# Attention products with v in column tiles of 32, and sums of both heads in the same rows

## The chip, the cores and the metric

The kernel runs on one core of one Trainium2 chip. The metric is the device time of one execution in microseconds; the kernel before has a median of 639.19 us over three runs (638.57 to 639.40).

## The reference

Three layers follow one another. The diff touches only the first, attention over 2 x 8 heads of width 64 with 576 pooled queries and 1152 keys a head; its output goes through a routed expert layer and a last gated layer.

```python
q_pool = q.reshape(B, H, S // 2, 2, D).mean(axis=3)
scores = np.matmul(q_pool, k.transpose(0, 1, 3, 2)) / np.sqrt(D)
scores = scores - np.max(scores, axis=-1, keepdims=True)
attn = np.exp(scores)
attn = attn / (np.sum(attn, axis=-1, keepdims=True) + 1e-09)
x = np.matmul(attn, v)
...
x = moe(x)
...
out = (h * np.tanh(softplus(h))) @ w_out      # h = x @ w_in
```

## The kernel before

Attention handles the 16 heads as 8 pairs (p = 0 to 7), and the keys of a pair as 9 tiles of 128 (t = 0 to 8). The main loop runs over the 72 steps (p, t). Each step issues the scores of its tile (keys on partitions, queries along the free dimension, lines 320 and 322), ACT exponentiates them into the tile `Pt[p, t]`, and some matmuls of the next pair's row maxima stand between (`max_chunk`, lines 237 and 241). All orders are written out by hand; each engine runs its instructions in that order.

The products with v don't run at every step. `groups` collects three tiles: at steps 0, 3 and 6 the products of the three tiles before are issued. At step 0 they are the last three of the pair before, and its end. In the last pair groups have two tiles, at steps 2, 4, 6 and 8, and the last tile stands alone behind the loop.

`pv(p, t, f)` multiplies exp(scores) of half f of the 576 queries with v: for each of the two heads, one matmul with 128 keys as contraction, 64 columns of weights (the width of v) and 288 queries as the moving operand. Head h writes rows 64h to 64h + 63 of PSUM bank f (`pvt[p][f]`), columns 0 to 287. VectorE adds the tiles of a group into `St`, and `psums` then sums exp(scores) over the keys: matmuls whose weights are `e2[:, h]`, 32 columns, all zero but column h, which is one. They write columns 288 to 447 of the same banks, 160 queries at a time. Operands are float32.

At the end of a pair `evac_x` lets ACT copy the products of bank f out of PSUM (the tile is `wd` in the trace), `evac_s` lets ACT copy the sums of the second head, and `sum_both` lets VectorE add the sums of the first head onto them (`sm`), so that both heads' sums stand in one set of rows. `sum_log` (line 401, weights of 32 columns) forms gate products at step 3 (step 4 in the last pair) between products and sums; at step 6 the transposes of the next pair's maxima stand there (`max_rows`, lines 287 and 289). `sum_tr` transposes `sm` at step 6.

Line numbers: 339 is the matmul of `pv`, 371 that of `psums`, 473 the transposes of the finished products; 90 (ACT) and 93, 96, 99, 102 (VectorE, POOL) are helpers.

Of the kernel before, what the change touches and what calls it, by code (L numbers as in the profile page):

```python
# [15 lines left out]
ALU = mybir.AluOpType  # L16
# [5 lines left out]
B, H, S, D = 2, 8, 1152, 64  # L22
SQ = S // 2
HQ = SQ // 2
# [6 lines left out]
KT = S // P  # L31
# [52 lines left out]
def kernel(ctx, tc, cst, qt, kt, v, wgo, w1, w2, wio, out):  # L84
    nc = tc.nc
    V, A, G, T, SP = nc.vector, nc.scalar, nc.gpsimd, nc.tensor, nc.sync
    mm = T.matmul

    def act(out, in_, func=AF.Copy, **kw):
        A.activation(out=out, in_=in_, func=func, **kw)  # L90

    def tt(eng, out, a, b, op):
        eng.tensor_tensor(out=out, in0=a, in1=b, op=op)  # L93
# [55 lines left out]
    sm = ap.tile([P, 384], F32, name="sm")  # L149
# [8 lines left out]
    kd, qd, vt, At, QS, QB, xut = {}, {}, {}, {}, {}, {}, {}  # L158
    Pt, pvt = {}, {}
# [68 lines left out]
    def max_chunk(p, h, j, c):  # L228

        pool, name = (mxp, "mx") if p or c == 0 else (scp, "sc")  # L230
        ps = pool.tile([P, 512], F32, name=name)[:, :KC]

        def keys(g_):
            return KD[p, g_] if c == 1 else At[p, g_][:, c * KC:(c + 1) * KC]

        if j < 4:
            mm(ps, lhsT=QS[p, h][:, j * P:(j + 1) * P], rhs=keys(h), start=True, stop=True)  # L237
        else:

            for g_ in range(2):  # L240
                mm(ps, lhsT=QM[p % 2][:, g_ * P:(g_ + 1) * P], rhs=keys(g_), start=g_ == 0, stop=g_ == 1)
        if c == 0:
            red(Mp[p % 2][:, h, j, 0:1], ps, ALU.max)
        elif c == 1:

            i, nrl[0] = nrl[0] % 3, nrl[0] + 1
            rlt[p, h, j] = wd[13 + i][:, (640, SQ, 0)[i]:(640 + KC, SQ + KC, KC)[i]]
            act(rlt[p, h, j], ps, AF.Relu)
        else:
            r_ = rlt.pop((p, h, j))  # L250
            V.tensor_tensor_reduce(out=r_, in0=ps, in1=r_, scale=1.0, scalar=-3.0e38, op0=ALU.add, op1=ALU.max, accum_out=Mp[p % 2][:, h, j, 1:2])  # L251
# [8 lines left out]
    def step_chunks(p, t):  # L260

        if p == 0 and t < 6:
            return [(1, *units[u], c) for u in FIRST[t] for c in (0, 2)], [(1, *units[u], 1) for u in FIRST[t + 1]]
        n, u = (p + 1, t + 3) if t < 6 else (p + 2, t - 6)
        if n >= NPAIR:
            return [], []
        unit = lambda i, c: (n, *units[i], c)
        if t % 3 == 0:
            post = [unit(u, 0), unit(u, 2), unit(u + 2, 1)]
            return [unit(u, 1), unit(u + 1, 1)], [post[i] for i in ((0, 2, 1) if t == 6 else (0, 1, 2))]  # L270
        return [unit(u, 0), unit(u, 2)], []
# [29 lines left out]
    last = NPAIR - 1  # L301
# [8 lines left out]
    def scores(p, t):  # L310
        ks = slice(t * P, (t + 1) * P)
        Pt[p, t] = ap.tile([P, 2, SQ], F32, name="pt", bufs=4)
        pool, name = (mxp, "mx") if other(p, t) else (scp, "sc")
        s0 = pool.tile([P, 512], F32, name=name)
        s1 = [pool.tile([P, 512], F32, name=name)[:, :SQ - F0] for h in range(2)]
        lo, hi = slice(0, F0), slice(F0, SQ)

        def part(o, h, qs_, low, first=True, last_=True):
            if low:
                mm(o, lhsT=Bt[(2 * p + h) % NBL][:66, ks], rhs=QB[p, h][:66, qs_], start=False, stop=last_, skip_group_check=not (first and last_))  # L320
            else:
                mm(o, lhsT=At[p, h][:, ks], rhs=QS[p, h][:, qs_], start=first, stop=False, skip_group_check=not (first and last_))  # L322

        for low in (False, True):
            part(s1[0], 0, hi, low)
        act(Pt[p, t][:, 0, F0:], s1[0], AF.Exp, scale=0.0625)
        for low in (False, True):
            for h in range(2):
                part(s0[:, h * F0:(h + 1) * F0], h, lo, low, h == 0, h == 1)
        act(Pt[p, t][:, :, :F0], s0.rearrange("p (h n) -> p h n", h=2), AF.Exp, scale=0.0625)  # L330
        for low in (False, True):
            part(s1[1], 1, hi, low)
        act(Pt[p, t][:, 1, F0:], s1[1], AF.Exp, scale=0.0625)

    def pv(p, t, f):
        if t == 0 and f == 0:
            pvt[p] = [pvp.tile([P, 512], F32, name=f"pv{i}") for i in range(2)]
        for h in range(2):
            mm(pvt[p][f][64 * h:64 * h + 64, :HQ], lhsT=vt[p][:, t, h, :], rhs=Pt[p, t][:, h, f * HQ:(f + 1) * HQ], start=t == 0, stop=t == KT - 1, skip_group_check=True)  # L339


    St = {}
# [1 line left out]
    def groups(p, t):  # L344

        if p == last and t:
            return [(last, i) for i in range(t - 2, t)] if t % 2 == 0 else []
        g = 9 * p + t
        return [divmod(i, KT) for i in range(g - 3, g)] if t % 3 == 0 and g else []

    def add_tile(tiles):
        p = tiles[0][0]
        if len(tiles) > 1:
            St[p] = ap.tile([P, 2, SQ], F32, name="st", bufs=1)
            tt(V, St[p], Pt[tiles[0]], Pt[tiles[1]], ALU.add)
            if whole(tiles):
                tt(V, St[p], St[p], Pt[tiles[2]], ALU.add)

    def whole(tiles):
        return len(tiles) == 3 and tiles[0] != (0, 0)  # L360

    def psums(tiles):
        p = tiles[0][0]
        srcs = [St[p]] * (len(tiles) > 1) + [Pt[tiles[-1]]] * (len(tiles) != 2 and not whole(tiles))
        end = tiles[-1][1] == KT - 1
        for f in range(2):
            for src in srcs:
                for h in range(2):
                    for a in range(2):
                        q_, t0 = 64 * h + 32 * a, 256 * a + 160 * f  # L370
                        mm(pvt[p][f][q_:q_ + 32, HQ:HQ + 160], lhsT=e2[:, h], rhs=src[:, h, t0:t0 + 160], start=False, stop=end and src is srcs[-1], skip_group_check=True)

    def evac_x(p, f):
        b, hp = divmod(p, 4)
        xu = xut[p] = wd[14][:, :SQ]
        act(xu[:, f * HQ:(f + 1) * HQ], pvt[p][f][:, :HQ])
        if f:
            o = 512 if b == 0 else 0
            G.tensor_copy(xu4[:, hp, 64 * b:64 * b + 64], xu[:, o:o + 64])

    def evac_s(p):
        b = p // 4
        sr = sm[64:, 64 * b:64 * b + 320].rearrange("p (f n) -> p f n", f=2)
        for f in range(2):
            act(sr[:, f], pvt[p][f][64:, HQ:HQ + 160])

    def sum_both(p):
        b = p // 4
        sr = sm[64:, 64 * b:64 * b + 320].rearrange("p (f n) -> p f n", f=2)
        for f in range(2):  # L390
            tt(V, sr[:, f], pvt[p][f][:64, HQ:HQ + 160], sr[:, f], ALU.add)

    rct, slt = {}, {}

    def sum_log(p, out=True):

        b, hp = divmod(p, 4)
        ps = bank(now[0])
        for a in range(2):
            qs_ = slice(256 * a, 256 * a + 320)  # L400
            mm(ps[32 * a:32 * a + 32, :320], lhsT=wbd[:, hp], rhs=xut[p][:, qs_], start=True, stop=True)
        slt[p] = ps
        if out:
            evac_l(p)

    def evac_l(p):
        b = p // 4
        act(sm[:64, 64 * b:64 * b + 320], slt[p][:64, :320])
# [184 lines left out]
    for p in range(NPAIR):  # L593
        n, m = p + 1, p + 2
# [144 lines left out]
    def run(g, slot):  # L739
        for f in sched.get((g, slot), ()):  # L740
            f()

    for g in range(9 * NPAIR):
        p, t = divmod(g, 9)
        now[0] = g
        scores(p, t)
        run(g, 0)
        pre, post = step_chunks(p, t)
        for c_ in pre:
            max_chunk(*c_)  # L750
        tiles = groups(p, t)
        if tiles:
            add_tile(tiles)
        run(g, 1)
        end = tiles and tiles[-1][1] == KT - 1
        for f in range(2):
            for i in tiles:
                pv(*i, f)
            if end:
                evac_x(p - 1, f)  # L760
        if t == 6 and p < last:
            max_rows(p + 1)
        if p and t == (4 if p == last else 3):
            sum_log(p - 1)
        if tiles:
            psums(tiles)
        run(g, 4)
        if end:
            evac_s(p - 1)
        run(g, 2)  # L770
        for c_ in post:
            max_chunk(*c_)
        if end:
            sum_both(p - 1)
        run(g, 3)
    psums([(last, KT - 1)])
    for f in range(2):
        pv(last, KT - 1, f)
        evac_x(last, f)
    sum_log(last, False)  # L780
    evac_s(last)
    sum_both(last)
    evac_l(last)
    sum_tr(last)
    sum_last(last)
# [543 lines left out]
    for q, (n_, i, _, main, w_, _) in enumerate(flat):  # L1329
# [39 lines left out]
        elif wq and (n_ == 5 and i % 2 or n_ == 6 or n_ == 7 and i < 4) and len(ws2) < NPRE:  # L1369
            f = len(ws2)  # L1370
# [300 lines left out]
```

## Time and profile before

| | |
|---|---|
| median of three runs | 639.19 us |
| profiled execution | 640.59 us |
| its span, first to last instruction | 638.8 us |
| mean granted TensorE clock | 0.988 |
| TensorE busy (PE) | 612.3 us, 96% |
| VectorE (DVE) | 500.6 us, 78% |
| ScalarE (ACT) | 393.1 us, 62% |
| GpSimd (POOL) | 256.4 us, 40% |

PE is the matmuls, PEld the weight loads beside them. Busy times of records that overlap are counted once. The attention stage lasts to about 258 us of the span.

### The profile page before, as it was taken

To read this page: it belongs to the slowest core of one execution; us is meant where nothing else is said; L and a number is where in the kernel's file an instruction comes from. 1 tells how busy PE (TensorE), PEld (TensorE's weight loads), DVE (VectorE), ACT (ScalarE), POOL (GpSimd) and SP (SyncE) were. 2 spreads that over 40 slices of the span, in tenths; PEclk is the share of its full clock that TensorE was granted. 3 is DMA by queue.
4 is the path that set the end of the run, shared out by engine and by line. 5 is a ranking of instruction groups with operands and counts; after the bars stand their busy time and mean duration, and the time that the engine had idled before them with its cause. 6 is when DMAs were issued, how large, how long until landed. Compare 5 with 4: busy or idle time off the path is not lost.

```text
span 638.8 us, 11233 instructions
## 1 busy us (share of the span) xinstructions
PE 612.3 (96%) x4041; PEld 488.3 (76%) x4041; DVE 500.6 (78%) x1018; ACT 393.1 (62%) x855; POOL 256.4 (40%) x236
## 2 busy tenths in 40 slices
PE   8999999999999999599999989999999999999996
PEld 4677877768777766289868768597979998999993
DVE  7769798888888888558846768757898778878775
ACT  7888888888887674244555465844654545554453
POOL 6766738565566342242215132103323332223221
PEclk9999999999999999699999999999999999999999
DMA  8685745555451321498797694920000200010001
GB/s 325 201 230 186 214 144 126 159 148 192 91 177 48 111 89 65 142 334 295 267 388 265 239 374 195 331 73 2 0 1 1 100 2 1 2 43 7 1 0 54
DMA packets 27341, 89.73 MB, mean 140 GB/s; under 512 B 2854, under 2 KB 7599, under 8 KB 23186
## 3 DMA queue, kind: packets, MB, share of 16 engines
q1 hardware_dynamic: 22176, 74.80, 33.0%
q0 software_dynamic: 3504, 8.65, 5.9%
q10 hardware_dynamic: 1602, 5.51, 2.6%
q8 instruction: 34, 0.56, 0.4%
q14 instruction: 25, 0.20, 0.1%
HBM read 79.51 MB, written 9.84 MB: 140 GB/s over the span
## 4 chain that ended last, share of the span: by engine, by line
PE 65%; DVE 16%; ACT 8%; issue 4%; DMA 4%; POOL 1%; SPq 0%; ACTq 0%; DVEq 0%
PE pv L339 10%; PE ops L1489 8%; PE mx L237 5%; PE sc L322 5%; PE sc L320 5%; DVE l L96 4%; PE zps L1027 3%; PE zps L1028 3%; PE zps L1029 3%; PE yp L1027 2%; PE yp L1029 2%; PE yp L1028 2%; DVE n L96 2%; ACT l L90 2%; PE hps L1196 2%
## 5 line engine op out<-in xcount | busy, mean ns | idle before, releaser
L99 POOL TENSOR_SCALAR u<-u 128x384 f32<-128x384 f32 x46 | 58.8, 1279 | 143.5 <-ACT u L90 136.6
L90 ACT ACTIVATE pt<-sc 128x320 f32<-128x320 f32 (+1 forms) x198 | 87.9, 491 | 10.1 <-PE sc L320 7.6
L90 ACT ACTIVATE l<-n,two 128x384 f32<-128x384 f32 x48 | 29.6, 616 | 80.5 <-DVE n L96 80.5
L339 PE MATMUL pv<-pt,vt 128*64 128x288 f32 x576 | 75.6, 411 | 0.0
L322 PE MATMUL sc<-qs,at 128*128 128x320 f32 (+1 forms) x264 | 67.3, 299 | 0.0
L320 PE MATMUL sc<-qb,Bt 66*128 66x320 f32 (+1 forms) x264 | 66.6, 296 | 0.0
L339 PEld LDWEIGHTS pv<-pt,vt 128*64 128x64 f32 x576 | 39.0, 137 | 28.5 <-issue 5.2
L102 DVE TENSOR_REDUCE Mp<-mx 128x1 f32<-128x384 f32 x72 | 39.9, 556 | 24.9 <-PE mx L237 19.5
L1028 PE MATMUL zps<-yh,wd 128*128 128x384 f32 x176 | 59.1, 336 | 0.0
L1489 PE MATMUL ops<-wd,gh 128*128 128x512 f32 x135 | 53.2, 394 | 0.0
L99 POOL TENSOR_SCALAR dm<-dm 128x512 f32<-128x512 f32 x21 | 42.8, 2039 | 22.7 <-ACT dm L90 22.6
L96 DVE SCALAR_TENSOR_TENSOR l<-n,r 128x384 f32<-128x384 f32 x48 | 26.7, 557 | 31.1 <-ACT r L90 31.1
L322 PEld LDWEIGHTS sc<-qs,at 128*128 128x128 f32 x264 | 46.1, 189 | 1.0 <-issue 0.8
L93 POOL TENSOR_TENSOR Bt<-kd,at 64x576 fp32r<-64x576 f32 x32 | 46.3, 1461 | 0.2
L320 PEld LDWEIGHTS sc<-qb,Bt 66*128 66x128 f32 x264 | 45.3, 189 | 0.0
L93 DVE TENSOR_TENSOR w2l<-wt,w2h 128x512 fp32r<-128x512 f32 x32 | 25.9, 815 | 15.9 <-ACT w2h L90 15.7
L237 PE MATMUL mx<-at,qs 128*128 128x384 f32 x120 | 36.1, 369 | 1.5 <-DVE qs L93 0.8
L93 DVE TENSOR_TENSOR st<-pt 128x1152 f32<-128x1152 f32 x25 | 35.8, 1431 | 1.3 <-ACT pt L90 1.3
L1065 POOL DMA_INDIRECT ybuf<-y,six x11 | 11.2, 1020 | 63.7 <-ACT y L90 62.1
L93 DVE TENSOR_TENSOR n<-n,l 128x384 f32<-128x384 f32 x48 | 34.8, 725 | 1.7
L251 DVE CUSTOM_DVE_ANT_0 wd<-mx,wd 128x384 f32<-128x384 f32 x63 | 34.6, 550 | 1.8 <-PE mx L237 1.6
L1028 PEld LDWEIGHTS zps<-yh,wd 128*128 128x128 f32 x176 | 33.0, 188 | 1.5
(364 smaller groups left out, 1719.2 us busy)
## 6 DMA issues: line engine op xcount, KB each, us to landing
wt<-in_w SPq DMA_DIRECT2D x32, 1024.0 KB, 8.0
kd<-in_kt SPq DMA_DIRECT2D x16, 576.0 KB, 5.2
wraw<-in_wio SPq DMA_DIRECT2D x11, 512.0 KB, 4.5
wd<-in_wio SPq DMA_DIRECT2D x11, 512.0 KB, 4.1
vt<-in_v SPq DMA_DIRECT2D x8, 576.0 KB, 6.3
wraw<-in_wio ACTq DMA_DIRECT2D x7, 512.0 KB, 5.4
tq<-in_qt SPq DMA_DIRECT2D x12, 288.0 KB, 4.4
tq<-in_qt POOLq DMA_DIRECT2D x12, 288.0 KB, 6.4
```

The lines of the kernel that those rows point to most:

```text
L90: A.activation(out=out, in_=in_, func=func, **kw)
L93: eng.tensor_tensor(out=out, in0=a, in1=b, op=op)
L96: V.scalar_tensor_tensor(out=out, in0=a, scalar=s, in1=b, op0=op0, op1=op1)
L99: eng.tensor_scalar(out=out, in0=a, scalar1=s1, scalar2=s2, op0=op0, op1=op1)
L102: V.tensor_reduce(out=out, in_=in_, axis=AX.X, op=op)
L237: mm(ps, lhsT=QS[p, h][:, j * P:(j + 1) * P], rhs=keys(h), start=True, stop=True)
L251: V.tensor_tensor_reduce(out=r_, in0=ps, in1=r_, scale=1.0, scalar=-3.0e38, op0=ALU.add, op1=ALU.max, accum_out=Mp[p % 2][:, h, j, 1:2])
L320: mm(o, lhsT=Bt[(2 * p + h) % NBL][:66, ks], rhs=QB[p, h][:66, qs_], start=False, stop=last_, skip_group_check=not (first and last_))
L322: mm(o, lhsT=At[p, h][:, ks], rhs=QS[p, h][:, qs_], start=first, stop=False, skip_group_check=not (first and last_))
L339: mm(pvt[p][f][64 * h:64 * h + 64, :HQ], lhsT=vt[p][:, t, h, :], rhs=Pt[p, t][:, h, f * HQ:(f + 1) * HQ], start=t == 0, stop=t == KT - 1, ...
L1028: mm(out_, lhsT=b_, rhs=c, start=False, stop=False)
L1489: mm(opt[b_, j], lhsT=(g_, g_, gl_)[i], rhs=(wo, wl_, wo)[i], start=f == 0 and i == 0, stop=f == NF - 1 and i == 2)
```

## The change

Each product with v is split into two of 32 weight columns, so the four column tiles of bank f are written by head 0 and head 1 with two each. In `psums` the loop over bank f moves inside the loop over the head, and the row block of a sum is chosen by the bank (64 f) and no longer by the head (64 h): both heads add into the same rows, where the weights keep them in different rows of the block. `evac_s` therefore reads rows 64 f of bank f, and `sum_both` is dropped with both of its calls.

```diff
         for h in range(2):
-            mm(pvt[p][f][64 * h:64 * h + 64, :HQ], lhsT=vt[p][:, t, h, :], rhs=Pt[p, t][:, h, f * HQ:(f + 1) * HQ], start=t == 0, stop=t == KT - 1, skip_group_check=True)
+            for d in range(0, D, 32):
+                mm(pvt[p][f][64 * h + d:64 * h + d + 32, :HQ], lhsT=vt[p][:, t, h, d:d + 32], rhs=Pt[p, t][:, h, f * HQ:(f + 1) * HQ], start=t == 0, stop=t == KT - 1, skip_group_check=True)
...
-        for f in range(2):
-            for src in srcs:
-                for h in range(2):
+        for src in srcs:
+            for h in range(2):
+                for f in range(2):
                     for a in range(2):
-                        q_, t0 = 64 * h + 32 * a, 256 * a + 160 * f
+                        q_, t0 = 64 * f + 32 * a, 256 * a + 160 * f
                         mm(pvt[p][f][q_:q_ + 32, HQ:HQ + 160], lhsT=e2[:, h], rhs=src[:, h, t0:t0 + 160], start=False, stop=end and src is srcs[-1], skip_group_check=True)
...
-            act(sr[:, f], pvt[p][f][64:, HQ:HQ + 160])
-
-    def sum_both(p):
-        b = p // 4
-        sr = sm[64:, 64 * b:64 * b + 320].rearrange("p (f n) -> p f n", f=2)
-        for f in range(2):
-            tt(V, sr[:, f], pvt[p][f][:64, HQ:HQ + 160], sr[:, f], ALU.add)
+            act(sr[:, f], pvt[p][f][64 * f:64 * f + 64, HQ:HQ + 160])
...
-        if end:
-            sum_both(p - 1)
...
-    sum_both(last)
```

## Rows read from the trace of the kernel before

**Rows 1.** The page: TensorE's busy time, and the chain's shares by line.
```profile
PE 612.3 (96%) x4041; PEld 488.3 (76%) x4041; DVE 500.6 (78%) x1018; ACT 393.1 (62%) x855; POOL 256.4 (40%) x236
...
PE pv L339 10%; PE ops L1489 8%; PE mx L237 5%; PE sc L322 5%; PE sc L320 5%; DVE l L96 4%; PE zps L1027 3%; PE zps L1028 3%; PE zps L1029 3%; PE yp L1027 2%; PE yp L1029 2%; PE yp L1028 2%; DVE n L96 2%; ACT l L90 2%; PE hps L1196 2%
```

**Rows 2.** Windows of attention: stretch, length, busy us (count) of PE, PEld, DVE, ACT, POOL; clock.
```profile
26.00:228.00 202.00, 198.14 (x1608) 149.87 (x1606) 171.28 (x377) 166.69 (x387) 120.97 (x110) 1.00 0.52 153
228.00:256.00 28.00, 27.83 (x270) 18.59 (x269) 24.50 (x46) 15.12 (x36) 9.18 (x5) 1.00 0.30 92
```

**Rows 3.** Waits of TensorE, 26 to 256 us: total us, times, longest.
```profile
PE mx L237 <- ACT qb L90: 1.3, 6, 0.2
...
PE mx L237 <- DVE Mp L102: 0.3, 1, 0.3
```

**Rows 4.** Lines 339 and 371: records, ns min/median/max, first and last start.
```profile
L339 PE MATMUL pv<-pt,vt x576: 406/406/458, 30.0 to 255.7; 128*64 128x288 f32 x192
...
L371 PE MATMUL pv<-st,e x400: 299/299/324, 33.1 to 253.8; 128*32 128x160 f32 x134
```

**Rows 5.** Time line of TensorE, first sums: start, length, record count.
```profile
33.35 0.45 PE L371 MATMUL pv<-pt,e 128*32 128x160 f32 x8
...
33.89 0.46 PE L371 MATMUL pv<-pt,e 128*32 128x160 f32 x8
```

**Rows 6.** Time line of TensorE, a pair's end (step 0).
```profile
110.16 3.13 PE L339 MATMUL pv<-pt,vt 128*64 128x288 f32 x24
113.22 0.48 PE L371 MATMUL pv<-st,e 128*32 128x160 f32 x8
113.86 0.48 PE L371 MATMUL pv<-st,e 128*32 128x160 f32 x8 [0.16 <-ACT wd L90]
```

**Rows 7.** The last round of the products in that group.
```profile
112.88 0.41 PE L339 MATMUL pv<-pt,vt 128*64 128x288 f32 x2
```

**Rows 8.** Time line of TensorE at a step 3.
```profile
122.38 0.47 PE L371 MATMUL pv<-st,e 128*32 128x160 f32 x4
122.64 0.44 PE L401 MATMUL mx<-wd,wbd 128*32 128x320 f32 x2
```

**Rows 9.** Time line of TensorE at a step 6.
```profile
103.50 0.75 PE L371 MATMUL pv<-st,e 128*32 128x160 f32 x16
...
104.84 0.44 PE L237 MATMUL mx<-kx,qs 128*128 128x384 f32 x1 [0.21 <-ACT qb L90]
```

**Rows 10.** Time line of ACT at the end of that pair.
```profile
113.40 0.41 ACT L90 ACTIVATE wd<-pv 128x288 f32<-128x288 f32 x1 [1.10 <-PE pv L339]
...
115.12 0.49 ACT L90 ACTIVATE wd<-mx 128x384 f32<-128x384 f32 x1 [0.21 <-PE mx L237]
```

**Rows 11.** VectorE's additions of the sums, by shape: busy us, mean ns, idle before.
```profile
L93 DVE TENSOR_TENSOR sm<-pv,sm 64x160 f32<-64x160 f32 x16 | 4.5, 314 | 3.0 <-ACT sm L90 2.9
```

**Rows 12.** The chain of the last pair: start, length, what.
```profile
232.51 0.68 ACT dm L90
...
236.28 2.44 POOL dm L99
238.74 0.44 DVE dm L99
...
251.90 1.36 DVE st L93
...
253.31 0.75 PE pv L371 x16
```

**Rows 13.** Time line of all engines at the end of attention.
```profile
254.25 0.75 PE L371 MATMUL pv<-pt,e 128*32 128x160 f32 x16
254.93 1.19 PE L339 MATMUL pv<-pt,vt 128*64 128x288 f32 x8
...
256.94 0.55 DVE L93 TENSOR_TENSOR sm<-pv,sm 64x160 f32<-64x160 f32 x2 [2.29 <-ACT sm L90]
...
257.47 0.43 ACT L90 ACTIVATE sm<-sc 64x320 f32<-64x320 f32 x1 [0.38 <-PE sc L401]
```

## The prediction

> **What bounds the kernel now.** I read the page's engine line first, then the windows around the attention stage (the only stage that the diff touches), the waits of TensorE in it, the chain, and last the time line of TensorE around each kind of group. The page says that TensorE is busy for 96% of the span and that the line of the products with v holds 10% of the chain [rows 1]. The windows split attention in two. From 26 to 228 us TensorE works 198.1 of 202.0 us at a granted clock of 1.00, and nothing else is as full; from 228 to 256 us, the last pair of heads, it is again full, but VectorE is at 24.5 of 28.0 [rows 2]. The largest kind of wait that TensorE has in all these 230 us comes to 1.3 us [rows 3]. So up to 228 us a nanosecond saved or added on TensorE moves everything behind it; after 228 us the chain has to be asked again (below).
>
> **How the product groups run.** 8 pairs x 9 key tiles x 2 halves x 2 heads are 288 matmuls of the program; the trace has 576 records of them, so each leaves two [rows 4], and records of two column tiles run side by side. The lengths 406 ns for 288 columns and 299 ns for 160 [rows 4] differ by 107 ns for 128 columns, 0.836 ns a column: 288 columns stream in 241 ns, 160 in 134. A group of three key tiles starts at 110.16, its last round at 112.88 [rows 6, 7]: 11 intervals, less 0.052 (458 - 406) for the uncovered first weight load [rows 4], give 0.2425 us a round of two records: streaming and 2 ns. The sums already use four column tiles of 32. Rows of two rounds each start at 33.35 and 33.89, four rounds apart [rows 5]: 0.135 us a round of four records, again streaming and some 2 ns. Hence four streams side by side cost no more than two.
>
> **Part 1, tiles of 32 columns.** The records double to 1152, but four now share a round: 1152/4 = 576/2 = 288 rounds of the same 288 columns. Change: 0, on the evidence of the sums' rounds. The doubled issuing is covered too: the two-source sums issue 16 matmuls of the program in 8 rounds of 0.135 (one in 68 ns), while the new products need 24 in 12 rounds of 0.2425 (one in 121 ns). Not shown is a round of four with 288 columns: the bound below is 0, as nothing can stream faster; above, I take the start stagger as uncovered, 28 - 14 ns more a round. That stagger I get from the first two rows of the sums: the records of rows 4 with 299 ns give a two-round row of 0.45 (0.135 + 0.299 + three staggers), so about 7 ns each; 288 x 14 ns = 4.0 us. I take 0, the row that is nearest in kind.
>
> **The switch that goes.** From the last round of the products (112.88) to the first of the sums (113.22) pass 0.34 us [rows 6, 7], a round and 0.10 more. Where both have 32 columns I take that 0.10 away, and the sums' uncovered first load, 324 - 299 = 25 ns [rows 4]. The products' own uncovered first load falls from 52 ns to what 32 columns cost in the sums, 25: 27 ns less. A group whose products are followed directly by 32-column work gains 0.10 + 0.025 + 0.027 = 0.152 us. Of the 21 groups up to 228 us and at the start of the last pair, 7 are at step 3 of a pair (in six the gate product of line 401 stands between, also of 32 columns [rows 8]): 7 x 0.152 = -1.06. Seven are at step 6: between products and sums stand the transposes of the row maxima, 34 columns, so both switches stay and only 27 ns are gained (the wait on ACT's qb behind them [rows 9] follows the transposes, so it moves too): 7 x 0.027 = -0.19.
>
> **What the new order of the sums costs.** The other seven are at step 0, the end of a pair, and they wait. Before, the four sums of bank 0 run at once (113.22), then those of bank 1 wait until ACT has emptied the products of bank 1 (ACT 113.40 for 0.41) and start at 113.86 [rows 6, 10]. The new loop has bank inside head: two sums of bank 0, then two of bank 1 that wait for the same ACT instruction, and queued behind them on TensorE are the second head's two of bank 0 and two of bank 1. After the release there were 8 records in two rounds, 0.48 us [rows 6]. Now there are 12, and those of one bank lie in only two column tiles: head 0 then head 1 in bank 1 is four rounds in the same tiles, as long as a whole undisturbed group, 0.75 us [rows 9]. So 0.75 - 0.48 = +0.27, less the 0.027 of the first load: +0.245 a group. It can't be more, as four rounds are all the work there is; it would be 0 if TensorE took the later head around the held instruction. I take +0.27, because a waiting instruction is followed by nothing of its line in any of these groups.
>
> **Part 2, additions gone.** 16 additions on VectorE, 4.5 us busy [rows 11]. Up to 228 us TensorE waits for VectorE 0.3 us in all [rows 3], so they were hidden under its matmuls and free nothing; bounds 0 and -0.3. At the end of attention they run 256.94 to 257.49, while ACT copies the gate sums from 257.47 to 257.90 [rows 13], and the transposes need both: 0. ACT's two copies of the sums stay. The first now waits for the fourth round too, but ACT stood idle 0.21 us behind the copies, waiting for TensorE [rows 10], and that moves with TensorE: 0.
>
> **The last pair.** The chain there goes over ACT, POOL and VectorE, not TensorE: ACT's dm at 232.51 behind the copies of the sums, POOL's clamp 236.28 to 238.72, then from 238.74 to the addition at 251.90 thirty pieces, all VectorE's or its issuing; that addition releases the sums at 253.31 [rows 12]. The +0.245 of this pair's step 0 enters that chain through the copies of the sums; the gains of 0.152 at its steps 2, 4 and 6, and at 8 where VectorE is awaited, are eaten by it: 0 for the four. Behind it the last products follow sums directly: 254.93 - 254.25 is 0.68 [rows 13], against 0.54 for four rounds in one mode plus a first load 0.025: 0.115 gone, and 0.052 of first load with it: -0.165.
>
> **Sum.** -1.06 - 0.19 + 7 x 0.245 (1.72) - 0.165 = +0.30 us. The profiled execution took 640.59, its span 638.8 with 1.8 us around it: 640.9. It lay 1.40 above the median of the runs shown, 639.19, so I forecast a median of 639.5. About 0.2% (1.28 us) is what a measurement of this kernel can tell from no change.
>
> **Rivals.**
> - The hold at the end of a pair costs nothing, as TensorE runs the second head around the held sums. For it: behind line 401's first round four records of the sums start at 122.38 in other column tiles, before that line's second round [rows 8]. Against: those were not held by a wait. 7 x 0.27 less: 640.9 - 1.9 = 639.0, median 637.6, faster by 0.25%.
> - Rounds of four at 288 columns don't close up: the fourth stream's start stagger is added to each round. For it: no row shows four streams that long. Against: at 160 columns nothing is added. It decides from (1.28 - 0.30)/288 = 3.4 ns a round; at 14 ns, 639.5 + 4.0 = 643.5.
> - VectorE's freed 4.5 us are worth something in the last pair, where it is the chain. Against: it starts behind POOL there. Elsewhere TensorE waits 0.3 us for VectorE [rows 3], which I take as its bound: 639.2, within the likeliest's range.
>
> The Trainium skill, TensorEngine Tiling (Array Packing), section Instruction Overhead, says that each matmul carries about 60 cycles of overhead and warns of small ones; that speaks against doubling the count. At 2.4 GHz that is an estimate of 25 ns, for 576 added records 14.4 us if none of it is covered, 653.9; rounds of four that last 0.135 us [rows 5] don't show it.
>
> **Chances and range.** Likeliest (the sum) 0.69, by itself 638.7 to 640.4, which is the scatter of the runs (638.57 to 639.40) around it; no hold 0.12; rounds of four lengthened 0.10 (the uncovered overhead in it 0.02); the rest, 0.09, is a shift of ACT at pair ends that costs another 0.27 each (641.4), or small gains inside the likeliest's range. From 637.3 to 641.4 leaves out little more than the lengthened rounds. Faster by over 0.2%: 0.13; within: 0.69; slower: 0.18.
>
> **What would show it.** 1152 records of line 340 in 288 rounds of 0.2425; last products to first sums 0.24 instead of 0.34 at steps 3; at step 0 sums that end 0.27 later after ACT's evacuation; VectorE some 4.5 us less busy; span 638.8 + 0.3. Wrong if a round of four exceeds 0.246, if sums of the second head start before the evacuation ends, or if a pair's steps 1 and 2 wait for ACT where they didn't.

## The result, and the profile after

The changed kernel takes 642.98 us (median of 6 runs, 642.17 to 644.17), the kernel before beside it 638.85 (638.37 to 639.40): ratio 1.0064, 95% interval 1.0052 to 1.0077. The forecast was 639.5 within 637.3 to 641.4, so the time lies outside its range, on the slow side. The same kernel was measured four more times beside the kernel before, with ratios 1.0000, 1.0048, 1.0027 and 1.0047 (below). The mean of the five is 1.0037, some 2.4 us: the change loses, but by less than its first measurement says.

The page of the changed kernel, its engine line and two DMA queues (queue, kind: packets, MB, share):

```profile
PE 611.6 (95%) x4617; PEld 487.6 (76%) x4617; DVE 493.8 (77%) x1002; ACT 393.2 (61%) x855; POOL 257.4 (40%) x236
...
q8 instruction: 38, 0.62, 0.4%
q14 instruction: 25, 0.20, 0.1%
```

Against [rows 1] TensorE has 576 records more and less busy time, and VectorE 16 instructions and 6.8 us less. The two last lines I had passed over: transfers of the kind "instruction", 16 KB each on q8 and 8 KB on q14. They turn out to matter most.

The windows of attention in the changed kernel, to compare with [rows 2], and two behind attention:

```profile
26.00:228.00 202.00, 196.86 (x2084) 148.41 (x2082) 166.75 (x364) 166.11 (x386) 121.29 (x110) 1.00 0.52 153
228.00:256.90 28.90, 27.96 (x369) 18.97 (x369) 24.16 (x44) 16.00 (x38) 9.71 (x5) 1.00 0.28 89
272.00:276.00 4.00, 1.84 (x13) 1.39 (x12) 1.38 (x2) 1.20 (x2) 1.79 (x2) 0.93 0.83 244
276.00:280.00 4.00, 4.00 (x25) 4.00 (x24) 1.95 (x4) 1.63 (x3) 0.00 (x0) 0.63 0.78 235
```

TensorE now idles 5.1 us of the first 202 instead of 3.9. In the last two windows it stands idle for half of four microseconds and then works four at a granted clock of 0.63, a mixture of 1.2 and 2.4 GHz; in the kernel before the clock of 276 to 280 us is 1.00.

The lines of the products and the sums, for [rows 4]:

```profile
L340 PE MATMUL pv<-pt,vt x1152: 406/406/431, 30.0 to 256.5; 128*32 128x288 f32 x192
...
L372 PE MATMUL pv<-st,e x400: 299/299/324, 32.9 to 254.7; 128*32 128x160 f32 x134
```

TensorE's time line at the end of the pair of [rows 6], and at the step 3 behind it, for [rows 8]:

```profile
110.60 3.12 PE L340 MATMUL pv<-pt,vt 128*32 128x288 f32 x48
113.54 0.44 PE L372 MATMUL pv<-st,e 128*32 128x160 f32 x4
114.31 0.74 PE L372 MATMUL pv<-st,e 128*32 128x160 f32 x12 [0.33 <-ACT wd L90]
...
119.98 3.12 PE L340 MATMUL pv<-pt,vt 128*32 128x288 f32 x48
122.92 0.44 PE L396 MATMUL mx<-wd,wbd 128*32 128x320 f32 x2
122.93 0.47 PE L372 MATMUL pv<-st,e 128*32 128x160 f32 x4
```

From the first product to what follows pass 2.94 us (110.60 to 113.54, and 119.98 to 122.92): 12 rounds of 0.2425 and a first load of 0.03. Before it was 3.06 (110.16 to 113.22). The sums of bank 1 wait for ACT and 12 records follow in 0.74. Both are as the prediction had them. So the loss has to be elsewhere, and two places show it. The first stands between pair 0 and pair 1, on ACT's time line and then TensorE's, in the changed kernel:

```profile
42.44 0.70 ACT L90 ACTIVATE at<-kd 128x576 fp32r<-128x576 f32 x1
44.30 0.68 ACT L90 ACTIVATE qs<-tq 128x576 fp32r<-128x576 f32 x1 [1.16 <-DMA tq<-in_qt]
...
46.35 0.44 PE L237 MATMUL mx<-kx,qs 128*128 128x384 f32 x1 [0.67 <-ACT qb L90]
```

In the kernel before the same two rows are

```profile
43.44 0.68 ACT L90 ACTIVATE qs<-tq 128x576 fp32r<-128x576 f32 x1
...
46.06 0.44 PE L237 MATMUL mx<-kx,qs 128*128 128x384 f32 x1 [0.21 <-ACT qb L90]
```

ACT waits 1.16 us for the accumulating load of a query tile (`tq`, issued by POOL at 36.1), and hands the delay to TensorE's matmuls of the maxima. The second place is behind attention, at the first expert, which waits for gathered tokens; each row is the transposes of one of the first three gathered tiles, in the changed kernel:

```profile
271.81 0.75 PE L992 MATMUL xps<-cs,xg 128*128 128x128 f32 x4
273.02 0.63 PE L992 MATMUL yp<-cs,xg 128*128 128x128 f32 x4 [0.46 <-DMA xg<-xbuf,gix]
275.35 1.00 PE L992 MATMUL yp<-cs,xg 128*128 128x128 f32 x4 [1.71 <-DMA xg<-xbuf,gix]
```

and the third in the kernel before:

```profile
273.55 0.66 PE L1000 MATMUL yp<-cs,xg 128*128 128x128 f32 x4 [0.93 <-DMA xg<-xbuf,gix]
```

The second tile came 1.0 us later than in the kernel before (whose attention ended 0.8 us earlier), the third 1.8 us. The wait and the slow clock behind it are the two odd windows above.

### The profile page after: what moved, and what is told of

Its sections match the earlier page's. It is cut to its first block, busy times and chain, and to the rows that moved or that the text cites. A ratio compares the mean times of both kernels' runs of the same rounds, so it can differ in the third digit from the quotient of the medians.

```text
span 642.0 us, 12368 instructions
## 1 busy us (share of the span) xinstructions
PE 611.6 (95%) x4617; PEld 487.6 (76%) x4617; DVE 493.8 (77%) x1002; ACT 393.2 (61%) x855; POOL 257.4 (40%) x236
## 4 chain that ended last, share of the span: by engine, by line
PE 60%; DVE 17%; ACT 8%; DMA 7%; issue 5%; POOL 2%; SPq 0%; ACTq 0%; DVEq 0%; POOLq 0%
PE pv L340 8%; PE ops L1481 8%; PE sc L322 4%; PE sc L320 4%; DVE l L96 4%; PE mx L237 4%; PE zps L1019 3%; PE zps L1020 3%; PE zps L1021 3%; DMA tq<-in_qt 2%; DVE n L96 2%; PE yp L1019 2%; PE yp L1021 2%; PE yp L1020 2%; ACT l L90 2%
## 5 line engine op out<-in xcount | busy, mean ns | idle before, releaser
L340 PE MATMUL pv<-pt,vt 128*32 128x288 f32 x1152 | 75.2, 408 | 0.0
L340 PEld LDWEIGHTS pv<-pt,vt 128*32 128x32 f32 x1152 | 34.9, 110 | 31.5 <-issue 4.7
L99 POOL TENSOR_SCALAR dm<-dm 128x512 f32<-128x512 f32 x21 | 43.2, 2057 | 22.5 <-ACT dm L90 22.4
L237 PE MATMUL mx<-at,qs 128*128 128x384 f32 x120 | 36.1, 369 | 1.2 <-DVE Mp L102 0.6
L93 DVE TENSOR_TENSOR w2l<-wt,w2h 128x512 fp32r<-128x512 f32 x32 | 24.5, 771 | 12.0 <-ACT w2h L90 11.8
```

The source lines that it names most:

```text
L99: eng.tensor_scalar(out=out, in0=a, scalar1=s1, scalar2=s2, op0=op0, op1=op1)
L340: mm(pvt[p][f][64 * h + d:64 * h + d + 32, :HQ], lhsT=vt[p][:, t, h, d:d + 32], rhs=Pt[p, t][:, h, f * HQ:(f + 1) * HQ], start=t == 0, sto ...
```

## The experiments

Eighteen kernels ran. The starts of the groups of products in each profile were set against those of the kernel before; "end of attention" is the first of the last pair's own gate products, behind the loop (256.63 us before, 257.45 after; "the first gate product" below), counted from pair 0's step 3, so that differences of the loads at the start drop out.

**Halves of the change, and an early guess.** `e1` has the products of 32 columns with the old sums; `e2` the new sums with products of 64; `e3` is the kernel before, with 28 matmuls of 64 columns more ahead of its last products.

```diff
 # e2, against the changed kernel
-            for d in range(0, D, 32):
-                mm(pvt[p][f][64 * h + d:64 * h + d + 32, :HQ], lhsT=vt[p][:, t, h, d:d + 32], ...
+            mm(pvt[p][f][64 * h:64 * h + 64, :HQ], lhsT=vt[p][:, t, h, :], ...
 # e3, against the kernel before
+    for _ in range(7):
+        for q_ in range(0, P, 32):
+            mm(pvt[last][0][q_:q_ + 32, 448:], lhsT=e2[:, 0], rhs=Pt[last, KT - 1][:, 0, :64], ...)
```

> Products in tiles of 32 columns, sums and additions as before. Theory A (the loss has two parts: the sums of bank 1 held at the pair ends, and a loss of 2 to 3 us behind attention that depends only on when attention ends): every group keeps its gain and none pays the longer hold, so the last gate product of attention, 256.63 us before, comes at about 255.1, and the time is 636.5 to 638.5. Theory B (column tiles of 32 cost something by themselves that the attention stage does not show, for instance through the doubled instruction stream): attention ends as early, but the time stays above that of the kernel before, about 641.

> Products in tiles of 64 columns as before, sums by bank and half with both heads in the same rows, no additions. Theory A: seven pair ends pay 0.27 us each and nothing is gained, so the last gate product comes at about 258.5 instead of 256.63, and the time is 641 to 643. Theory B: the attention stage is later by the same 1.9 us, but nothing is lost behind it, 640.8.

> The kernel before with 28 matmuls of 64 columns into unused columns ahead of the last products, so attention ends 0.8 us later and nothing else is changed. Theory A: behind attention 2 to 3 us more are lost, as in the changed kernel, and the time is 641.5 to 643. Rival: a shift passes through as it is, 639.7; then the 2 to 3 us behind attention come from something else in the change.

Measured: `e1` 637.81 us, 0.9987 [0.9969, 1.0004]; `e2` 642.02, 1.0042 [1.0029, 1.0055]; `e3` 639.70, 1.0000 [0.9990, 1.0010]. At the end of attention `e1` is 0.39 us ahead of the kernel before and `e2` 1.74 behind. So the new order of the sums is what costs within attention (+0.25 at each of seven pair ends, as predicted), and the tiles of 32 gain, but less than the 1.4 us of their terms: ACT's wait for `tq` is 1.44 us in `e1`, 0 in `e2`. `e3`'s third gather came late too, without any part of the change, and yet its time is the one that the rival gives: the shift of 0.65 us passes through as it is.

**Where ACT's copies stand.** `e4` puts both copies of the products behind the sums, `e6` only that of bank 1.

```diff
 # e4, against the changed kernel
-            if end:
-                evac_x(p - 1, f)
+        if end:
+            for f in range(2):
+                evac_x(p - 1, f)
 # e6
-            if end:
+            if end and f == 0:
...
+        if end:
+            evac_x(p - 1, 1)
```

> The changed kernel with the sums at a pair's end issued ahead of both evacuations of the products, so no sum waits for ACT. By the attention terms each of seven pair ends gains the whole hold, about 0.6 us against the changed kernel: the last gate product comes at about 253.5 instead of 257.45, 3 us ahead of the kernel before, and the time is 636 to 638 if the later stages follow. If ACT, which now evacuates in one go at the pair's end, becomes the bound there, half of that is lost and waits of TensorE for ACT show at steps 0 and 1.

> The changed kernel, but at a pair's end only the evacuation of bank 1 is issued behind the sums; that of bank 0 stays between the halves of the products, where ACT is free. No sum waits for ACT then. TensorE gains 0.63 us at each of seven pair ends against the changed kernel; if ACT, which now works 0.4 us later there, holds the next scores, half of it is lost. The last gate product of attention comes between 253.3 and 255.5 us (257.45 in the changed kernel, 256.63 before); the time is 636 to 638.5, below the kernel before.

Measured: `e4` 641.12 us, 1.0028 [1.0017, 1.0039]; `e6` 641.95, 1.0036 [1.0020, 1.0052]. Neither can be told from the changed kernel's own measurements, and attention ends no earlier (258.57 and 259.03 us): in `e4` ACT stands idle 1.85 us at a pair's end, and is late for what follows.

**The changed kernel again, and warm matmuls.** `e5` is the changed kernel unaltered; `e7` gives TensorE six small matmuls to do while it waits for the third gathered tile.

```diff
 # e7
+            if s == slots[0][0] and j == 2:
+                for _ in range(6):
+                    mm(pr, lhsT=one16, rhs=ohr[:, :8].rearrange("p t r -> p (t r)"), start=True, stop=True)
```

> The changed kernel once more, timed on one chip beside the two below. Its attention stage ends 0.8 us later than before, and a bare shift of 0.65 us cost 0.55 us, the sums alone 2.2 us later cost 2.9. Theory C (the loss is the shift of attention, and the rest of the first 4.1 us was the spread of the later stages from execution to execution): 639.7 to 641.5, 1 to 2 us above the kernel before. Theory D (the changed kernel as a whole, both parts together, loses 2 to 3 us behind attention): 642.5 to 643.5, 4 us above.

> The changed kernel with six more idle matmuls between the second and the third gathered tile of the first expert, where TensorE was idle for 1.7 us and its granted clock then fell to half for some 2.5 us. If the late third gather costs through the clock, the stretch from the last gate product of attention to the first expert matmuls falls from 18.6 to 17.5 us or the following matmuls run at the full clock, and the time is 1.5 to 2 us below that of the changed kernel beside it. If the gather itself is what later stages wait for, or they take back what is lost there, the time is the same within 0.5 us.

Measured: `e5` 640.32 us, 1.0000 [0.9987, 1.0014]; `e7` 640.45, 1.0007 [0.9993, 1.0022]. In this measurement the changed kernel loses nothing that can be told, and ACT's wait in its profile is the smallest of the changed kernel's five, 0.38 us. The warm matmuls can't be told from it either.

**Copies.** `e8` and `e9` are the changed kernel, `e10` the kernel before, `e11` is `e1`: no edit at all.

> The changed kernel, first of two identical copies, beside a copy of the kernel before. The first measurement gave the changed kernel 4.1 us more, the second, on another chip, 0.2. Theory E (a constant of one loading of a program, such as where its buffers lie: executions of one loading agree, two loadings of the same program differ): the two copies differ from one another by 2 us or more, and so may the copy of the kernel before from the kernel before. Theory F (a property of the chip or of the time at which it was measured): the two copies agree within 0.5 us, and both stand either 0 to 1 us or 3 to 5 us above the kernel before. The attention stage alone says 0.8.

> The changed kernel, second identical copy: theory E, 2 us or more away from the first; theory F, within 0.5 us of it.

> The kernel before, an identical copy: theory E, 1 us or more away from the kernel before; theory F, within 0.5 us of it.

> Products in tiles of 32 columns with the sums and additions as before, once more: 1.3 us below the kernel before in its first measurement. If that was the gain of the attention stage it comes back between 0.5 and 1.8 us below; under theory E it can lie anywhere within 2 us of the kernel before.

Measured: 641.95, 641.15, 639.68 and 637.41 us; 1.0048 [1.0030, 1.0066], 1.0027 [1.0014, 1.0041], 1.0004 [0.9992, 1.0016] and 0.9965 [0.9955, 0.9976]. The copy of the kernel before is where it should be, the copies of the changed kernel differ by less than its measurements on other occasions do (0.8 us, which meets neither theory), and the tiles of 32 with the old sums are faster than both kernels, by more than was expected (2.2 us by the ratio).

**Whose wait is it?** `e12` to `e14` choose the width of the column tiles for pair 0 alone; `e15` is the changed kernel once more.

```diff
+        w = 64 if p == 0 else 32          # e12, e14;  e13: 32 if p == 0 else 64
         for h in range(2):
-            for d in range(0, D, 32):
-                mm(pvt[p][f][64 * h + d:64 * h + d + 32, :HQ], lhsT=vt[p][:, t, h, d:d + 32], ...
+            for d in range(0, D, w):
+                mm(pvt[p][f][64 * h + d:64 * h + d + w, :HQ], lhsT=vt[p][:, t, h, d:d + w], ...
```

> The changed kernel, but pair 0's products keep weight tiles of 64 columns (the other seven pairs have 32). Nine profiles with products of 32 columns show ACT waiting 0.4 to 2.0 us for the accumulating load of tq between pair 0's step 6 and pair 1's step 0, four with 64 columns 0 to 0.4 us. Theory G (the products of 32 columns that run just then hold that load back): ACT's wait at most 0.4 us, the start of pair 1's first group at +0.0 to +0.1 us against pair 0's last instead of +0.44, and a time about 0.5 us below the changed kernel of the same job. Theory H (it is the program as a whole, wherever the small tiles stand): wait of 1 to 2 us as before, same time as the changed kernel. Theory R (chance of the executions): no pattern over this run and the next two.

> The kernel before, but pair 0's products (and only they) have weight tiles of 32 columns; sums and additions as before. Theory G: ACT waits 0.4 to 2 us for tq between pair 0 and pair 1, and pair 1's first group starts 0.4 to 1 us later against pair 0's last; time of before, 0.3 (two switches gone, -0.18, three first loads -0.08) less and 0.5 more: +0.2 us. Theory H: no wait, time of before less 0.3 us. Theory R: either.

> The kernel with products of 32 columns and the sums of before, but pair 0's products in 64 columns. Theory G: no wait above 0.4 us for tq, and against the kernel before -2.2 us (the same with all pairs in 32 columns measured 0.9965 on one chip) less another 0.5 us plus 0.2 for pair 0's own switches: about -2.5 us, 0.996. Theory H and R: -2.0 us, 0.997.

> The changed kernel unchanged, beside the three above. Its four measurements so far gave 1.0064, 1.0000, 1.0048 and 1.0027. By the mean of these +2.2 us, 1.0035; ACT's wait for tq 0.4 to 1.5 us.

Measured: `e12` 641.51 us, 1.0042 [1.0024, 1.0060]; `e13` 639.01, 0.9997 [0.9988, 1.0007]; `e14` 638.63, 0.9989 [0.9978, 0.9999]; `e15` 642.46, 1.0047 [1.0030, 1.0064]. ACT's wait is 0.61, 1.33, 0.21 and 0.93 us; pair 1 starts +0.01, +0.63, +0.03 and +0.19 against pair 0's last group. The later start goes with tiles of 32 in pair 0, the wait less clearly (`e12`'s 0.61 is above the 0.4 of theory G). But the tiles are not the only thing that changes there. The transfers between 36 and 44 us, by queue, in the changed kernel:

```profile
q1 hardware_dynamic: 589, 1.50, 63.4%
q0 software_dynamic: 150, 0.31, 22.4%
q8 instruction: 1, 0.02, 1.1%
```

and in the kernel before, in the same stretch:

```profile
q1 hardware_dynamic: 591, 1.51, 64.1%
q0 software_dynamic: 144, 0.29, 21.8%
```

One packet of instructions lies in the flight of the load. The packets' own times in the trace (us from the span's start) sort all the kernels; q0 closes a load with 16 small writes, the last two of which are shown:

```
                        q8 packets near          15th, 16th write   ACT waits
before                  27.5   44.5   57.6       43.04   43.05      0
e12 (pair 0 in 64)      28.8   44.7   58.1       43.22   43.51      0.61
e14 (pair 0 in 64)      28.2   44.2   55.8       42.84   42.98      0.21
after                   28.3   41.4   53.3       42.90   43.95      1.16
e13 (only pair 0 in 32) 28.2   41.5   52.7       42.98   44.05      1.33
e11 (old sums)          28.6   42.1   53.4       42.96   44.14      1.48
e17 (below)             15.8   33.5   45.6       42.83   42.92      0.40
```

Fifteen parts of the load land by 42.8 to 43.2 us in all of these; where the packet falls into the flight, the sixteenth is 1.0 to 1.2 us behind (0.7 to 1.6 over the twelve profiles of that kind, 0.01 to 0.34 over the eight others). From 28 us to the end of attention q8 has on average a packet for every 253 or 254 records of TensorE, matmuls and weight loads together (15 intervals over 3816 records before, 19 over 4802 after), and the doubled products bring the second of them forward from 44.5 to 41.4.

q14 has the same story for VectorE: from 205 us to the end seven of its packets lie 125 to 132 of VectorE's records apart. Where VectorE has its old number of instructions, one lies 8.31 us behind the first gate product of the last pair, and 2 within the last 6 us of the span (ten profiles); with the 16 additions gone the first moves to +15 or +16 or isn't found, and 3 lie at the end (ten profiles). One more packet of q14 lies at +15.8 to +16.7 in all twenty, so what the change adds there is a second one.

**Moving the packets.** `e16` gives VectorE 16 additions of one column at the places of the old ones, results unused. `e17` also cuts 19 matmuls of the warm-up at the start into four each, which puts 114 records more ahead in TensorE's program; `e18` does this cut to `e1`.

```diff
 # e16, e17, against the changed kernel
+    def v_pad():
+        for _ in range(2):
+            tt(V, gsc[:, :1], ones, ones, ALU.add)
...
+        if end:
+            v_pad()
...
+    v_pad()
 # e17, e18
-            mm(w, lhsT=one16, rhs=one16.unsqueeze(1).to_broadcast([P, 4, P]), start=True, stop=True)
+            for i in range(parts):
+                j = 4 // parts
+                mm(w[:, i * j:i * j + j], lhsT=one16, rhs=one16.unsqueeze(1).to_broadcast([P, j, P]), start=True, stop=True)
```

> The changed kernel with two additions of 128x1 elements on VectorE at each place where the old kernel added the sums of a pair (16 in all, results unused), so that VectorE's program is as long as before. Theory I (fetches of instructions): the trace has packets of 8 KB on q14, kind instruction, that fall about every 128 instructions of VectorE; with 16 instructions fewer, one that fell 8.3 us behind the first gate product of the end of attention falls at +15.2 to +16.2, into the landing of the third gather, which then lands 0.4 to 0.9 us later, and another falls into the last stores. With the padding it goes back to +8.3: first gate product to first expert 17.2 to 17.4 us instead of 18.2 to 18.6 (five profiles of the changed kernel), first zps to the end 215.4 instead of 216.1 (their mean); time 1.0 to 1.7 us below the changed kernel, whose five measurements average 1.0037, so 1.0010 to 1.0021. Rival S (scatter of clock and gathers): 18.2 to 18.6 stays, ratio 1.0037.

> As e16, and 19 of the warm-up matmuls at the start, 512 columns each, cut into four of 128, so that 57 instructions more (114 records with their weight loads) lie ahead in TensorE's program. Theory I: packets of 16 KB on q8, kind instruction, fall about every 256 records of TensorE; in the kernels with 32 columns in pair 0 one falls at 38 to 42.7 us, into the flight of the load of tq (36 to 43), whose last of sixteen parts then lands 0.7 to 1.7 us behind the fifteenth; shifted by 114 records it falls at 32 to 35 us, and the wait of ACT goes to 0.4 us or less, pair 0's last group to pair 1's first +0.0 to +0.1 us. Time another 0.5 us below e16: 1.0002 to 1.0013. Theory G (the column tiles themselves hold the load back): ACT's wait stays at 0.4 to 2 us, time of e16.

> Products of 32 columns with the sums, copies and additions of before, and the warm-up matmuls cut as in e17. That arrangement without the cut measured 0.9987 and 0.9965 (ACT's wait for tq 1.44 and 1.48 us). Theory I: the wait goes to 0.4 us or less, first gate product to first expert stays at 17.3, and the time is about 0.5 us less: 0.9957 to 0.998. Theory G: wait and time as without the cut.

Measured: `e16` 647.24 us, 1.0114 [1.0091, 1.0137]; `e17` 648.16, 1.0124 [1.0098, 1.0149]; `e18` 639.19, 0.9991 [0.9977, 1.0005]. The times miss all expectations, the places meet them. The gathered tiles in `e16`:

```profile
280.16 1.06 PE L999 MATMUL xps<-cs,xg 128*128 128x128 f32 x4
281.42 0.63 PE L999 MATMUL yp<-cs,xg 128*128 128x128 f32 x4 [0.19 <-DMA xg<-xbuf,gix]
282.72 0.66 PE L999 MATMUL yp<-cs,xg 128*128 128x128 f32 x4 [0.67 <-DMA xg<-xbuf,gix]
```

The third starts 1.30 us behind the second, not 2.33 as in the changed kernel. From the last pair's first gate product to the first expert pass 17.33 us in `e16` and 17.20 in `e17`; in the five profiles of the changed kernel it is 18.16 to 18.56 (mean 18.35), in the nine with VectorE's old count but `e3`, these two among them, 17.20 to 17.41 (mean 17.30). At the end of the program, the packets of q14 in the last 10 us of the span, in the changed kernel and then in `e16`:

```profile
q14 instruction: 3, 0.02, 0.6%
```

```profile
q14 instruction: 2, 0.02, 0.6%
```

The issue of the last store in the time lines of the changed kernel (span 642.0 us) and of `e16` (645.3):

```profile
636.66 0.35 ACTq L1488 DMA_DIRECT2D out<-o  x1
```

```profile
641.32 0.35 ACTq L1495 DMA_DIRECT2D out<-o  x1
```

From this issue to the end of the span pass 5.36 and 3.99 us. Over the ten profiles with three packets there it is 4.21 to 5.36 (mean of the changed kernel's five: 4.64), over the ten with two 3.75 to 4.50 (mean 3.96). And with TensorE's packet at 33.5 and 34.4 us ACT waits 0.40 and 0.38 us for `tq` in `e17` and `e18`, and pair 1 starts +0.01 and -0.01, with tiles of 32 in pair 0; the last two writes of the load are 0.09 and 0.10 us apart. So it is the packets, not the tiles.

Why then 8 us more? The padding itself. VectorE's and POOL's time lines in `e16` at a pair's end, and VectorE's in the last pair:

```profile
119.62 2.63 DVE L93 TENSOR_TENSOR gsc<-cs 128x1 f32<-128x1 f32 x2
...
240.58 0.34 DVE L93 TENSOR_TENSOR gsc<-cs 128x1 f32<-128x1 f32 x2
```

```profile
119.44 2.80 POOL L93 TENSOR_TENSOR Bt<-kd,at 64x576 fp32r<-64x576 f32 x2
```

An addition of a single column takes 0.15 us where POOL is idle (four of the 16) and 1.25 to 1.35 where POOL subtracts 64x576 elements (twelve): each of the twelve ends within 0.03 us of one of POOL's subtractions. VectorE is then late with the maxima, and TensorE waits for it 5.7 us in five places of attention, which ends 8.3 us later than in the changed kernel. The additions that the change removed took 0.31 us at the same place [rows 11]; they read one operand from PSUM. That this difference is the reason was not tried by itself.

`e18`'s wait went as expected, and its attention ends 1.02 us ahead of the kernel before, where `e1` and `e11` are 0.4 ahead. Its time did not fall with it: 0.9991 against 0.9965 and 0.9987 for `e1`'s arrangement. Half a microsecond is less than these differ among themselves. So the packets are shown to set the places of these delays; that the delays make up the loss of the changed kernel is not shown by any time.

**The granted clock of the executions.** The mean granted clock of each execution is on record, and it sorts those of the changed kernel: 20 have 0.989 or less and take 642.7 us on average, 22 have 0.990 or more and take 640.4. Of the five measurements, in the order of their ratios above, the lower clock has 6 of 6 executions, 0 of 11, 4 of 6, 5 of 12 and 5 of 7; of the kernel before, in the later measurements, 24 of 149. A low mean doesn't tell where the clock fell (the profile of the kernel before has 0.988, with a fall at 380.7 us), but the profiles of the changed kernel do. TensorE waits 1.71 us for the third gathered tile in the changed kernel's first profile and in `e5`'s; then it works at 1.2 GHz in the one and at 2.4 GHz in the other, here from 276 to 278.8 us:

```profile
276.00:278.80 2.80, 2.80 (x15) 2.80 (x14) 1.78 (x4) 1.63 (x3) 0.00 (x0) 0.50 0.74 260
```

```profile
276.00:278.80 2.80, 2.80 (x23) 2.80 (x22) 1.92 (x5) 0.91 (x2) 0.00 (x0) 1.00 0.80 250
```

The profiles of `e8` and `e15` are as the first, that of `e9` as the second. From the first gate product to the first product of the last layer (`zps`) pass 166.5 to 168.0 us in those three and 164.8 and 165.6 in the other two; in the nine kernels with an early third tile and VectorE's old count it is 164.1 to 168.7 (mean 165.9). So in these profiles the late tile costs time further on where the clock falls behind it, and none that can be told where it doesn't. Why it falls in three and not in two isn't known. In `e7`, whose matmuls fill the wait, the clock of this stretch is 1.00, and 1 of its 12 executions has a mean of 0.989 or less; but `e5` beside it has none, so the run had nothing to gain.

## Why the prediction was wrong

**Right: the rounds.** Four streams of 288 columns close up: 0.2425 us a round, 0.241 of it streaming. The rival of lengthened rounds is refuted. The Trainium skill, TensorEngine Tiling (Array Packing), section Instruction Overhead, gives about 60 cycles for each matmul, from which the prediction worked out its estimate of 14.4 us; no run here shows them uncovered.

**Right: the switch and the first loads.** Each group at step 3 gains 0.15 us. Each at step 6 gains 0.01 where 0.027 was forecast, about 0.09 in all instead of 0.19.

**Right: the hold.** TensorE doesn't run the second head around the held sums: +0.25 us at six of the seven pair ends and +0.15 at one, 1.7 in all, and +0.25 at each in `e2`, where it alone is left (1.74 us). The rival without hold falls.

**Right: the last pair.** What its steps 2, 4 and 6 gain (0.48 us in all) is given back at step 8, where TensorE waits 0.57 us for the addition into `st`; behind it 0.11 is gained where 0.165 was forecast.

Over these terms the five profiles of the changed kernel end attention 0.89 us later than the kernel before (0.84, 0.38, 1.05, 1.43 and 0.74), of which 0.45 (mean; -0.01 to 1.01) arise in the one step from pair 0 to pair 1. The remaining 0.44 is the sum that was forecast as 0.30; the terms of step 6 and of the last pair are what it missed by.

**Wrong: what the number of instructions costs.** Two terms were put at nothing, by two sentences that failed. "The doubled issuing is covered too" was worked out for TensorE alone, and for TensorE it holds. But the doubled program is fetched by transfers of its own, and one of them now falls into the flight of the load of `tq`: +0.45 us. And of the 16 additions on VectorE the prediction said that "they were hidden under its matmuls and free nothing"; that is so as well, but without them VectorE's later packets come at other places: into the third gather, +1.05 us (18.35 - 17.30), and into the last stores, +0.69 (4.64 - 3.96). These costs lie where the prediction didn't look: it ended its sum at the end of attention, the only stage that the diff touches.

Added up, 0.44 + 0.45 + 1.05 + 0.69 = 2.6 us, where five measurements average 2.4. That the two agree is in part luck, for the terms are read at single places and not all of them reach the end: the spans of the five profiles average 639.7 us, 1.4 more than the two of the kernel before (638.8 and 637.9). Behind the first gate product the five take 382.6 us on average, the ten profiles with VectorE's old count 381.3 (379.5 to 384.0): 1.3 more, not 1.05 + 0.69. This excess stands in the three profiles whose clock fell behind the third tile (383.8) and not in the two others (380.9). So the 1.05 us at the first expert are not, as such, what reaches the end. What these profiles still show there is the clock that falls in some executions: between those with the lower and the higher mean clock lie 2.2 us (642.7 and 640.4). That the wait for the tile brings the fall about is likely but not shown.

Two pages of the Trainium skill bear on this. Runtime: NRT & Kernel Launch, section Instruction fetch mechanics, says that each engine's sequencer fetches its next block of instructions by its own DMA queue and that the cost is mostly hidden. Here the products' rounds show nothing of it, at 0.2425 us with either number of instructions, but the load of `tq` beside it does. The Trainium skill, DMA: Bandwidth & Descriptors, section Why a DMA increments its semaphore by 16 and not by 1, says that a transfer runs on up to 16 engines that finish independently and is complete only with all of them; the fifteenth and sixteenth writes at 42.90 and 43.95 us agree.

**Open.** The trace doesn't name the DMA engine of a packet, so that the late sixteenth part shares its engine with the fetch is an inference; that moving the packet removes the delay of `tq` is shown (`e17`, `e18`), and that VectorE's old count brings the third tile back (`e16`, `e17`). That the packet is the reason there, and at the last stores, rests on where the packets lie. The third tile is late in all eight profiles with two packets of q14 between +15.2 and +16.7 and early in eleven of the twelve with one there. `e3` is the twelfth: late (18.45 us), with its one packet at +16.6. `e2` and `e4`, with 16 instructions fewer, are early (17.42 and 17.26), the second packet of `e2` being at +15.0 and that of `e4` not found. The exact moment seems to decide, and a packet's moment shifts by some microseconds from one execution to the next (TensorE's second one: 38.2 to 42.7 us over the kernels with 32 columns in pair 0 and the warm-up uncut). That the first measurement gave 4.1 us and the second nothing goes with the clock, which was the lower one in all executions of the first and in none of the second, so that some 1.7 us of the 4.1 belong to that measurement alone; what decides the clock is open.

## What to carry to other kernels

Adding or removing instructions, even on an engine with time to spare, moves the fetches of its later instructions, and one that falls into the flight of a load that somebody waits for can make it land about 1 us later; how much of that reaches the end depends on what the waiting engine does next. Before a change of a few tenths of a microsecond is costed, look where the packets of kind "instruction" lie beside the transfers that somebody waits for. Giving such transfers a microsecond of slack should be safer than tuning the places of the packets, which drift; no run tried it. When executions of one kernel differ, sort them by their granted clock first. The part of this change that pays is the tiles of 32 columns alone, with the old order of the sums: 0.9965 to 0.9991 in four kernels (`e1`, `e11`, `e18`, and `e14`, which has tiles of 64 in pair 0), below 1 by its whole interval in two of them.

## What the runs showed of the hardware that was not expected

- Four float32 streams of 288 columns cost TensorE no more than two: 0.2425 us a round with either.
- An instruction of TensorE that waits holds back those behind it even if they write other column tiles and another bank: the sums of bank 0 of the second head stood behind the held ones of bank 1 at every pair end.
- VectorE's additions from SBUF into SBUF take longer beside POOL: one column took 1.25 to 1.35 us beside POOL's subtraction and 0.15 us without it. The Trainium skill, SBUF — State Buffer, section Terms, says that the two share a pair of ports which one holds for a whole instruction while the other is blocked; twelve ends within 0.03 us of POOL's agree.
- One packet of 16 KB of instructions (q8), which itself takes 0.9 to 1.5 us, goes with a delay of 0.7 to 1.6 us in the last sixteenth of a load of 288 KB.
